# Wider search products, an earlier third key copy and loads asked for at written steps

## The chip, the cores and the metric

The kernel runs on one core of one Trainium2 chip. The metric is the device time of one execution in microseconds; several runs are shown by their median.

## The reference

Three stages follow one another. x goes through all of them, 3072 tokens (4 sequences of 768) by 384 numbers.

```python
# 1: linear attention with decay, 8 heads of 48, for each sequence
for t in range(768):
    state = alpha[:, :, t, :, None] * state + k[:, :, t] (outer) v[:, :, t]
    y[:, :, t] = q[:, :, t] @ state
# 2: dense layer, 384 -> 2048 -> 384
h = np.maximum(x @ w_in, 0.0);  x = h * h @ w_out
# 3: eight experts, 384 -> 1024 -> 384, each with room for cap = 3072 // 8 tokens
order = np.argsort(-(x @ w_gate).flatten())
for idx in order:
    tok, e = idx // 8, idx % 8
    if assigned[tok] >= 0 or counts[e] >= cap: continue
    assigned[tok] = e; counts[e] += 1
out[mask] = np.maximum(x[mask] @ w1[e], 0.0) @ w2[e]     # mask: tokens of e
```

## The kernel before, in words

**Attention** goes by 24 chunks of 128 tokens, six for each sequence. A chunk is the generator `attn`, which is called piece by piece. Its pieces: "p" and "a", two scans on VectorE (L233, L237); "q", the scaled keys and queries kt and qt; then sad, the decayed state (GpSimd, L253), and the scores psc (TensorE, L260); for chunks from the fourth on, `turn` (transposed keys pn, which ScalarE copies to kn, L299), `mask` (VectorE, L266), `update` (pu, TensorE, L307), `keep` (the new state, VectorE, L316 or L318) and `result` (TensorE: L278 with the state, L281 with the masked scores; ScalarE copies it out). The first chunk of a sequence has no L278, the last one no update. At its "q" piece a chunk asks for the load of the chunk after the next (L247 to L249), chunks 3 to 5 on the sync engine (SP), later ones on ScalarE.

**The dense layer** goes by eight units of three chunks (384 tokens), each in 16 steps of 128 hidden columns. A step has nine matmuls of ph (L415), ScalarE's and VectorE's work to make hl (the first unit's last part is VectorE's, L431), and, two steps later, nine matmuls of p (L443). Every factor is kept as a sum of two numbers, so each product has three parts. In the first 16 steps the weights are converted as well: a pair of slices comes as 64-bit integers, VectorE takes three operations for it (L382, L384, L386), ScalarE and GpSimd split it. The 17 pairs, the first and last in halves, are begun by `start_conv` and finished by a later call.

**The order** on TensorE, VectorE, ScalarE and GpSimd is written by hand in two regions, as the text runs. In the opening, `ORDER` lists it: "w" is a small matmul that only keeps TensorE busy, "0p" or "2n" the next piece of one of the first three chunks, "C" starts a conversion, "S" finishes it, "L" asks for the pairs that are due, "x" splits the first unit's x (L353, L354). Then `first_step(g)` runs for g from 0 to 17: ph, the conversion's end, hl, the next conversion's start, p of two steps ago, and a piece each of chunks 3 to 6, which begin in the steps that `BEGIN` names. SP is not among these engines. From step 18 on the order is the framework's own; `piece` calls the later chunks at a set rate, skipping two of their halts.

**The experts.** For each of seven experts a search finds the lowest logit that still gets a place: five iterations, each of which narrows the range 32-fold. An iteration compares all logits with 32 thresholds (cm, VectorE), counts by expert (pc, six matmuls, L892), takes the counts over as rc, adds the four groups of 32 rows (pb by `same`, four matmuls, L905), asks where an expert would be full (VectorE), and counts these thresholds (pb by `later`, L910):

```python
for g in range(G):
    pe.matmul(pb[0:T, 0:E], same[:, g * T:(g + 1) * T], rc[:, g * E:(g + 1) * E], ...)
full = sm.tile([T, E], BF, name="full", bufs=2)
dve.tensor_tensor(full, pb[0:T, 0:E], cap[0:T], op=OP.is_ge)
pe.matmul(pb[:, E:2 * E], later, full, start=True, stop=True)
```

Here T is 32, G 4 and E 8. At the end of a search pz (L931) gives what was taken. Then GpSimd gathers the expert's weights (`load_w`, w1s and w2s), ScalarE and VectorE or GpSimd split them (L974, L976), the tokens are gathered and turned (L984), and layer 1 (ph, L1011) and layer 2 (py, L1029) run, nine and three times three matmuls a step. The search for expert e+1, the gathers and splits stand between them where `PLAN` puts them, again in an order written by hand. The first search stands in `START` between the last unit's p matmuls (L694).

Of the kernel before, what the change touches and what calls it, by code (L numbers as in the profile page):

```python
# [7 lines left out]
F32 = mybir.dt.float32  # L8
# [24 lines left out]
T = 32  # L33
# [8 lines left out]
def table(entries):  # L42
    at = {}
    for r, p, what in entries:
# [19 lines left out]
         "1 A t 99 t 1 s 1 t x h0 B r d0 h1 r d1 r h2 p2 r open r h3 r h4 p3 h5 r r r x h6 r p4 p5 r r r p6").split()  # L64
LEAD = 4
RATE = 15 / 16
ORDER = ("w w w w w w w w w w 0p 0a 0q 1p 0s 0n w w 1a 0o w w 1q 2p 1s 1n 2a 2q 1o w 2s C S C L 2n w w 2o x w w w w "
         "w w w w w w w w S C L w").split()

PAIRS = [((0, 0), (0, 1)), ((0, 2), (1, 0))] + [((0, f + 2), (1, f)) for f in range(1, FT - 2)] + [((1, 14), (1, 15))]  # L70

BEGIN = 1, 5, 8, 12
SPLIT = (14, 14, 15)
SB = 2
WF = 3
# [11 lines left out]
def moe_kernel(ctx: ExitStack, tc: tile.TileContext, akq, v, w_in, w_out, w_gate, w1, w2, out,  # L87
# [105 lines left out]
    pool.iota(iopc[:, :, 1], pattern=[[1, NCH]], base=0, channel_multiplier=0, allow_small_or_imprecise_dtypes=True)  # L193
    onesb = consts.tile([128, 128], BF, name="onesb")
    trim = consts.tile([128, 128], BF, name="trim")
    later = consts.tile([T, 128], BF, name="later")
    same = consts.tile([128, 128], F16, name="same")
    iopw = iota([128, 1], [[0, 1]], base=-128 * ID0, cm=1, name="iopw")
    sel = consts.tile([16, E], F32, name="sel")

    def late_consts():
        pool.memset(onesb, 1.0)
        dve.tensor_scalar(trim, jp, 0.0, -1.0, op0=OP.is_gt, op1=OP.add)
        dve.tensor_scalar(later, ones[0:T], iop[0:T], 0.5, op0=OP.mult, op1=OP.is_gt)
        dve.tensor_copy(same, ident)
        dve.tensor_scalar(sel, jp[0:16, 0:E], -float(E), None, op0=OP.is_equal)
        dve.tensor_tensor(sel, sel, ident[0:16, 0:E], op=OP.add)

# [10 lines left out]
    def attn(ch, tags="aaaaa"):  # L219
# [24 lines left out]
            ae = ap_.tile([112, NP], F32, name="ae", bufs=2)  # L244
            pool.tensor_copy(ae, P[:, :, 0])
        yield "q"
        if CPU <= ch < NCH - 2:  # L247
            load(ch + 2, eng=sp if ch < 2 * CPU else act)
            load_v(ch + 2, sp if ch < 2 * CPU else act)  # L249
        if c:  # L250
# [69 lines left out]
        if ch >= CPU:  # L320
            kn2 = turn()
            yield "s"
            mask(0, NP)
            yield "m"
            pu = None if last else update()
            yield "u"
            if not last:
                keep(pu)
            result(0, NP)
            yield "o"  # L330
            return
        if late:
# [178 lines left out]
    def loads():  # L511
        while due:
            load_pair(due.pop(0))
# [74 lines left out]
        return n  # L588

    def piece():  # L590
        if next(att, None) in ("s", "u"):
            next(att)

    def first_step(g):


        u, f = steps[g]
        for i, at in enumerate(BEGIN):
            if g - at in (4, 5):
                go(early[i])  # L600
        ph = bank("h", "ph")
        gated, asked = tasks[:], tasks[:]
        del tasks[:]
        moe_a(u, f, ph)
        for t in asked:
            t.send(ph)

        old, hi = before[:], before_gate[:]
        del before[:], before_gate[:]
        for t in hi:  # L610
            next(t)
        for e in old:
            go(e, 2)
        while begun:
            go(begun.pop(0))
        for e in old:
            go(e)
        start_conv()
        if g >= 2:
            moe_b(0, g - 2)  # L620
        for t in tasks:
            next(t)
        for i, at in enumerate(BEGIN):
            if 0 <= g - at <= 4:
                go(early[i])
        for i, w in enumerate(SPLIT):
            if g == w:
                split_x(1, (i,))
        before.append(moe_ev(u, f, ph, mp_.tile([128, 2, UT], F32R, name="hl", bufs=3)))
        before_gate.extend(gated)  # L630
        loads()

    before, before_gate = [], []
    early = [attn(CPU + i) for i in range(len(BEGIN))]
# [95 lines left out]
    pool.iota(iot[:, 0], pattern=[[1, T]], base=0, channel_multiplier=0, allow_small_or_imprecise_dtypes=True)  # L730
    for i in range(1, ITERS):
        act.activation(iot[:, i], iot[:, i - 1], AF.Copy, scale=1.0 / T)
    iol = sm.tile([T, 1], F32, name="iol")
    act.activation(iol, iop[0:T], AF.Copy, scale=float(T) ** (1 - ITERS))
    ioslot = sm.tile([128, CAP], F32, name="ioslot")
    pool.iota(ioslot, pattern=[[1, CAP]], base=-int(OFF), channel_multiplier=0, allow_small_or_imprecise_dtypes=True)
    IDX, XG, RW = {}, {}, {}
# [116 lines left out]
    def search(k):  # L854
# [21 lines left out]
        for it in range(ITERS):  # L876

            pc = bank("a", "pc")
            thr = iot[:, 0]
            if it:  # L880
                thr = pc[:, G * E:G * E + T]
                dve.tensor_scalar(thr, iot[:, it], n, at, op0=OP.add, op1=OP.add)
            cm = sm.tile([128, NCH, T], BF, name="cm", bufs=2)
            dve.tensor_tensor(cm, m2[:, :, None].to_broadcast([128, NCH, T]),
                              thr[:, None, :].to_broadcast([128, NCH, T]), op=OP.is_ge)
            if it == 0:
                oh = sm.tile(eb, BF, name="oh", bufs=2)
                dve.tensor_tensor(oh, L, m[:, :, None].to_broadcast(eb), op=OP.is_equal)
            yield

            for c in range(0, NCH, G):
                pe.matmul(pc[:, 0:G * E], cm[:, c:c + G].rearrange("p c t -> p (c t)"),  # L892
                          oh[:, c:c + G].rearrange("p c e -> p (c e)"), start=c == 0, stop=c == NCH - G)
            rc = sm.tile([128, G * E], F16, name="rc", bufs=2)
            dve.tensor_copy(rc, pc[:, 0:G * E])
            if it == 1:
                ee = sm.tile(eb, F32, name="ee", bufs=1)
                dve.tensor_tensor(ee, oh, ioe[:, None, :].to_broadcast(eb), op=OP.mult)
            if it == 2:
                ei = sm.tile([128, NCH], F32, name="ei", bufs=2)  # L900
                dve.tensor_reduce(ei, ee, axis=AX.X, op=OP.add)
            yield
            pb = bank("a", "pb")
            for g in range(G):
                pe.matmul(pb[0:T, 0:E], same[:, g * T:(g + 1) * T], rc[:, g * E:(g + 1) * E], start=g == 0,  # L905
                          stop=g == G - 1)
            full = sm.tile([T, E], BF, name="full", bufs=2)
            dve.tensor_tensor(full, pb[0:T, 0:E], cap[0:T], op=OP.is_ge)
            yield
            pe.matmul(pb[:, E:2 * E], later, full, start=True, stop=True)  # L910
            if it == 1:
                at = n
            elif 1 < it < ITERS - 1:
                at2 = sm.tile([128, 1], F32, name="at", bufs=2)
                dve.tensor_scalar(at2, at, n, None, op0=OP.add)
                at = at2
            n0, n = n, sm.tile([128, 1], F32, name="n", bufs=4)
            steps = sm.tile([128, E], F32, name="steps", bufs=1)
            dve.tensor_scalar(steps, pb[:, E:2 * E], float(T) ** -it, None, op0=OP.mult, op1=OP.max, accum_out=n)
            yield  # L920

        hi = sm.tile([128, 1], F32, name="hi", bufs=2)
        dve.tensor_scalar(hi, n, n0, at, op0=OP.add, op1=OP.add)
        taken = sm.tile([T, E], F32, name="taken", bufs=2)
        dve.scalar_tensor_tensor(taken, n[0:T].to_broadcast([T, E]), iol, pb[0:T, 0:E], op0=OP.is_equal, op1=OP.mult)
        a = pb[:, 2 * E:2 * E + NCH]
        dve.tensor_scalar(a, m2, hi, None, op0=OP.is_ge)
        dve.copy_predicated(aid, a.bitcast(mybir.dt.uint32), ei)
        yield
        pz = bank("a", "pz")  # L930
        pe.matmul(pz[:, 0:E], ones[0:T], taken, start=True, stop=True)  # L931
        cl = sm.tile([128, E], F32, name="cl", bufs=2)
        dve.tensor_tensor(cl, cap, pz[:, 0:E], op=OP.subtract)
        cz = sm.tile([128, E], F32, name="cz", bufs=2)
# [379 lines left out]
```

## Time and profile before

| what | value |
|---|---|
| three runs | 862.66, 857.23, 861.27 us; median 861.27 |
| the profiled execution | 859.59 us, of which the profile's span is 857.3 us |
| mean granted clock of TensorE | 0.978 of full |
| TensorE busy | 812.6 us (95% of the span) |
| VectorE busy | 493.4 us (58%) |
| ScalarE busy | 338.0 us (39%) |
| GpSimd busy | 361.7 us (42%) |

The stages in the trace: the opening to 31 us, the 18 written steps to about 128 us, the free steps to about 530 us, the last unit with the first search to some 590 us, and the experts. Busy shares over the whole span mix these stages. In the rows below, PE is TensorE, PEld its weight loads, DVE VectorE, ACT ScalarE, POOL GpSimd and SP the sync engine. A row of a timeline names start and length in us, engine, line, operation, what it writes and reads with their shapes, and behind x how many instructions it joins; in brackets the engine's idle time ahead of it and what ended it.

### The profile page before, as it was taken

The numbers are of one execution on the slowest core, as the hardware profiler recorded it, in microseconds if no ns is written. First come the engines' busy times: TensorE is split into PE (matmuls) and PEld (weight loads), VectorE is DVE, ScalarE is ACT, GpSimd is POOL, SyncE is SP. The second block draws the span as 40 slices with busy tenths as digits, with TensorE's granted clock in tenths as the row PEclk, the third lists the DMA queues.
The fourth block names the chain that finished last, engine by engine and source line by source line (L and its number), as shares of the span: only waits on it lengthen the run. The fifth ranks groups of instructions, "written<-read, shape, count | busy, mean of one in ns | idle before, by whom it ended". The sixth has DMA issues, their size and how long they took to land.

```text
span 857.3 us, 14404 instructions
## 1 busy us (share of the span) xinstructions
PE 812.6 (95%) x5752; PEld 755.4 (88%) x5752; DVE 493.4 (58%) x1091; ACT 338.0 (39%) x616; POOL 361.7 (42%) x351
## 2 busy tenths in 40 slices
PE   7889989999999999999999999986999999999993
PEld 6889989999999999999999999866887888889993
DVE  8899993434435434435443123477877876877730
ACT  2455644333233233234233245123445435536620
POOL 2466633342243342243343245134557577572511
PEclk8899989999999999999999999998999999999997
DMA  8555421112112102112100000041441532523500
GB/s 240 169 180 191 160 75 39 54 37 71 54 38 95 51 24 92 45 41 80 51 8 29 7 29 1 15 157 38 175 164 41 203 124 80 203 81 123 203 28 30
DMA packets 21625, 75.53 MB, mean 88 GB/s; under 512 B 3137, under 2 KB 10178, under 8 KB 19634
## 3 DMA queue, kind: packets, MB, share of 16 engines
q0 software_dynamic: 5520, 34.61, 11.0%
q1 hardware_dynamic: 11682, 25.72, 9.5%
q10 hardware_dynamic: 4352, 14.24, 5.5%
q8 instruction: 46, 0.75, 0.4%
q14 instruction: 25, 0.20, 0.1%
HBM read 63.84 MB, written 9.54 MB: 86 GB/s over the span
## 4 chain that ended last, share of the span: by engine, by line
PE 72%; DVE 15%; ACT 5%; issue 4%; DMA 2%; POOL 0%; POOLq 0%; SPq 0%; DVEq 0%; ACTq 0%
PE ph L415 20%; PE p L443 19%; PE ph L1011 9%; PE py L1029 7%; ACT wbuf L974 3%; DVE wf L384 3%; DVE wbuf L976 3%; PE psc L260 3%; PE py L281 3%; PE p L694 2%; PE py L278 2%; DMA w1s<-in_moe_w_dram,wi 2%; DVE wf L382 1%; PE pu L307 1%; PE pn L296 1%
## 5 line engine op out<-in xcount | busy, mean ns | idle before, releaser
L415 PE MATMUL ph<-xT,wbuf 128*128 128x384 f32 x1152 | 226.3, 340 | 4.5 <-DVE hl L431 4.5
L415 PEld LDWEIGHTS ph<-xT,wbuf 128*128 128x128 f32 x1152 | 203.8, 188 | 7.5 <-DVE hl L431 5.4
L443 PE MATMUL p<-wbuf,hl 128*128 128x392 f32 (+1 forms) x1008 | 203.7, 346 | 0.0
L427 DVE SCALAR_TENSOR_TENSOR s<-ph,s 128x384 f32<-128x384 f32 x112 | 62.4, 557 | 229.6 <-ACT s L420 229.2
L443 PEld LDWEIGHTS p<-wbuf,hl 128*128 128x128 f32 x1008 | 177.8, 189 | 4.0 <-issue 3.0
L431 POOL TENSOR_TENSOR hl<-s,hl 128x384 fp32r<-128x384 f32 x96 | 97.4, 1014 | 187.8 <-ACT hl L428 177.8
L420 ACT ACTIVATE s<-ph 128x384 f32<-128x384 f32 x128 | 63.0, 492 | 176.4 <-PE ph L415 141.3
L1029 PE MATMUL py<-wbuf,hl 128*128 128x384 f32 x576 | 125.2, 347 | 0.0
L1011 PE MATMUL ph<-xt,wbuf 128*128 128x384 f32 x576 | 117.1, 346 | 1.4 <-DVE xt L986 0.9
L1011 PEld LDWEIGHTS ph<-xt,wbuf 128*128 128x128 f32 x576 | 98.9, 188 | 5.0 <-DVE xt L986 2.3
L1029 PEld LDWEIGHTS py<-wbuf,hl 128*128 128x128 f32 x576 | 99.0, 188 | 0.7
L428 ACT ACTIVATE hl<-s 128x384 fp32r<-128x384 f32 x96 | 50.4, 525 | 73.9 <-DVE s L427 73.9
L1019 ACT ACTIVATE hl<-ph 128x384 fp32r<-128x384 f32 x64 | 31.5, 493 | 113.1 <-PE ph L1011 105.6
L400 POOL TENSOR_TENSOR wbuf<-wf,wbuf 128x384 fp32r<-128x384 f32 x32 | 42.1, 1334 | 33.3 <-ACT wbuf L399 33.3
L1020 DVE SCALAR_TENSOR_TENSOR hl<-ph,hl 128x384 fp32r<-128x384 f32 x64 | 35.5, 556 | 35.2 <-ACT hl L1019 35.2
L974 ACT ACTIVATE wbuf<-w1s 128x1024 fp32r<-128x1024 f32 x24 | 52.1, 2215 | 2.6 <-DMA w1s<-in_moe_w_dram,wi 2.6
L1037 POOL DMA_INDIRECT out_dram<-o,idx x24 | 28.7, 1197 | 51.6 <-ACT o L1034 19.7
L976 POOL TENSOR_TENSOR wbuf<-w2s,wbuf 128x768 fp32r<-128x768 f32 x24 | 43.5, 1837 | 5.6 <-ACT wbuf L974 5.6
L253 POOL TENSOR_TENSOR sad<-state,ae 48x192 f32<-48x192 f32 x40 | 24.6, 614 | 41.7 <-DVE state L316 29.3
L782 POOL DMA_INDIRECT xg<-x2d,row x24 | 22.9, 954 | 38.8 <-DVE idx L838 14.9
L976 POOL TENSOR_TENSOR wbuf<-w1s,wbuf 128x1024 fp32r<-128x1024 f32 x11 | 32.9, 3020 | 2.9 <-ACT wbuf L974 2.8
L260 PE MATMUL psc<-qt,kt 48*128 48x128 f32 x384 | 28.8, 291 | 3.4 <-DVE qt L242 3.4
(211 smaller groups left out, 1058.7 us busy)
## 6 DMA issues: line engine op xcount, KB each, us to landing
akq<-in_akq_dram ACTq DMA_DIRECT2D x16, 677.2 KB, 4.6
raw<-in_moe_w_in_dram SPq DMA_DIRECT2D x16, 384.0 KB, 3.1
raw<-in_moe_w_out_dram SPq DMA_DIRECT2D x16, 384.0 KB, 3.8
x2d<-xo SPq DMA_DIRECT2D x24, 192.0 KB, 2.0
akq<-in_akq_dram SPq DMA_DIRECT2D x6, 677.2 KB, 8.1
v<-in_v_dram ACTq DMA_DIRECT2D x16, 192.0 KB, 2.4
v<-in_v_dram SPq DMA_DIRECT2D x8, 192.0 KB, 4.9
xf<-xf SPq DMA_DIRECT2D x16, 72.0 KB, 2.6
```

Source lines behind the costliest of these rows:

```text
L260: pe.matmul(psc[j][:, p * 128:(p + 1) * 128], kt[o:o + D, p], qt[o:o + D, p], start=True, stop=True)
L400: pool.tensor_tensor(to[1], x, to[0].bitcast(F32), op=OP.subtract)
L415: pe.matmul(ph[:, :UT], win[:, wi, kt, fs], XT[u][:, xi, kt, :], start=n == 0, stop=n == 3 * KT - 1)
L420: act.activation(s, ph[:, :UT], AF.Relu)
L427: dve.scalar_tensor_tensor(s, ph[:, :UT], 0.0, s, op0=OP.max, op1=OP.mult)
L428: act.activation(hl[:, 0], s, AF.Copy)
L431: (dve if u == 0 or (u, f) == (NU - 1, FT - 1) else pool).tensor_tensor(hl[:, 1], s, hl[:, 0].bitcast(F32), op=OP.subtract)
L443: pe.matmul(PY[u][t][:, :w], hl[:, si, t * C:(t + 1) * C], wout[:, wi, f, :w], start=f == 0 and n == 0, stop=f == FT - 1 and n == 2)
L974: act.activation(dst[:, 0], src, AF.Copy)
L976: (dve if "d" in e else pool).tensor_tensor(dst[:, 1], src, dst[:, 0].bitcast(F32), op=OP.subtract)
L1011: pe.matmul(ph[:, :CAP], wa[:, wi, kt, j, :], xt[:, xi, kt, :], start=n == 0, stop=n == 3 * KT - 1)
L1029: pe.matmul(PX[k, i][:, :DM], hl[:, hi_, i * 128:(i + 1) * 128], wb[:, wi, j, :], start=j == 0 and n == 0, stop=j == FT2 - 1 and n == 2)
```

## The change

`ORDER` takes "2n" (the third chunk's transposed keys and their copy) ahead of the first two conversions, starts a third conversion behind "L" instead of far later, and has one "w" fewer there. The loads of chunks 7 and 8 leave the "q" pieces of chunks 5 and 6 and are asked for on SP at the end of steps 15 and 17. For chunks from the fourth on `result` goes ahead of `update`, and the halt between them is gone, so chunks 3 to 6 take six pieces where they took seven. In the search `same` and `later` have 128 columns and 128 rows: the sum over groups and all that follows stands in 128 rows, of which `later` uses the first 32; pz has 128 rows too. `same` becomes four matrices of 128 by 128, made by GpSimd ahead of the search.

```diff
@@ -64,12 +64,14 @@
          "1 A t 99 t 1 s 1 t x h0 B r d0 h1 r d1 r h2 p2 r open r h3 r h4 p3 h5 r r r x h6 r p4 p5 r r r p6").split()
 LEAD = 4
 RATE = 15 / 16
-ORDER = ("w w w w w w w w w w 0p 0a 0q 1p 0s 0n w w 1a 0o w w 1q 2p 1s 1n 2a 2q 1o w 2s C S C L 2n w w 2o x w w w w "
-         "w w w w w w w w S C L w").split()
+ORDER = ("w w w w w w w w w w 0p 0a 0q 1p 0s 0n w w 1a 0o w w 1q 2p 1s 1n 2a 2q 1o w 2s 2n C S C L C w 2o x w w w w "
+         "w w w w w w w w S L w").split()
 
 PAIRS = [((0, 0), (0, 1)), ((0, 2), (1, 0))] + [((0, f + 2), (1, f)) for f in range(1, FT - 2)] + [((1, 14), (1, 15))]
 
 BEGIN = 1, 5, 8, 12
+
+LATER = {7: 15, 8: 17}
 SPLIT = (14, 14, 15)
 SB = 2
 WF = 3
@@ -193,16 +195,17 @@
     pool.iota(iopc[:, :, 1], pattern=[[1, NCH]], base=0, channel_multiplier=0, allow_small_or_imprecise_dtypes=True)
     onesb = consts.tile([128, 128], BF, name="onesb")
     trim = consts.tile([128, 128], BF, name="trim")
-    later = consts.tile([T, 128], BF, name="later")
-    same = consts.tile([128, 128], F16, name="same")
+    later = consts.tile([128, 128], BF, name="later")
     iopw = iota([128, 1], [[0, 1]], base=-128 * ID0, cm=1, name="iopw")
     sel = consts.tile([16, E], F32, name="sel")
 
     def late_consts():
         pool.memset(onesb, 1.0)
         dve.tensor_scalar(trim, jp, 0.0, -1.0, op0=OP.is_gt, op1=OP.add)
-        dve.tensor_scalar(later, ones[0:T], iop[0:T], 0.5, op0=OP.mult, op1=OP.is_gt)
-        dve.tensor_copy(same, ident)
+
+        dve.tensor_scalar(scratch, iop, 0.5, None, op0=OP.is_gt)
+        dve.scalar_tensor_tensor(scratch, iop, T - 0.5, scratch, op0=OP.is_lt, op1=OP.mult)
+        dve.tensor_scalar(later, ones, scratch, None, op0=OP.mult)
         dve.tensor_scalar(sel, jp[0:16, 0:E], -float(E), None, op0=OP.is_equal)
         dve.tensor_tensor(sel, sel, ident[0:16, 0:E], op=OP.add)
 
@@ -244,7 +247,7 @@
             ae = ap_.tile([112, NP], F32, name="ae", bufs=2)
             pool.tensor_copy(ae, P[:, :, 0])
         yield "q"
-        if CPU <= ch < NCH - 2:
+        if CPU <= ch < NCH - 2 and ch + 2 not in LATER:
             load(ch + 2, eng=sp if ch < 2 * CPU else act)
             load_v(ch + 2, sp if ch < 2 * CPU else act)
         if c:
@@ -322,11 +325,10 @@
             yield "s"
             mask(0, NP)
             yield "m"
-            pu = None if last else update()
-            yield "u"
+
+            result(0, NP)
             if not last:
-                keep(pu)
-            result(0, NP)
+                keep(update())
             yield "o"
             return
         if late:
@@ -588,7 +590,7 @@
         return n
 
     def piece():
-        if next(att, None) in ("s", "u"):
+        if next(att, None) == "s":
             next(att)
 
     def first_step(g):
@@ -621,7 +623,7 @@
         for t in tasks:
             next(t)
         for i, at in enumerate(BEGIN):
-            if 0 <= g - at <= 4:
+            if 0 <= g - at <= 3:
                 go(early[i])
         for i, w in enumerate(SPLIT):
             if g == w:
@@ -629,6 +631,10 @@
         before.append(moe_ev(u, f, ph, mp_.tile([128, 2, UT], F32R, name="hl", bufs=3)))
         before_gate.extend(gated)
         loads()
+        for ch, at in LATER.items():
+            if g == at:
+                load(ch)
+                load_v(ch)
 
     before, before_gate = [], []
     early = [attn(CPU + i) for i in range(len(BEGIN))]
@@ -730,8 +736,12 @@
     pool.iota(iot[:, 0], pattern=[[1, T]], base=0, channel_multiplier=0, allow_small_or_imprecise_dtypes=True)
     for i in range(1, ITERS):
         act.activation(iot[:, i], iot[:, i - 1], AF.Copy, scale=1.0 / T)
-    iol = sm.tile([T, 1], F32, name="iol")
-    act.activation(iol, iop[0:T], AF.Copy, scale=float(T) ** (1 - ITERS))
+    iol = sm.tile([128, 1], F32, name="iol")
+
+    same = sm.tile([128, G, 128], F16, name="same")
+    pool.tensor_copy(same.rearrange("p g (r t) -> p g r t", t=T),
+                     ident.rearrange("p (g t) -> p g t", g=G)[:, :, None, :].to_broadcast([128, G, 128 // T, T]))
+    act.activation(iol, iop, AF.Copy, scale=float(T) ** (1 - ITERS))
     ioslot = sm.tile([128, CAP], F32, name="ioslot")
     pool.iota(ioslot, pattern=[[1, CAP]], base=-int(OFF), channel_multiplier=0, allow_small_or_imprecise_dtypes=True)
     IDX, XG, RW = {}, {}, {}
@@ -902,10 +912,10 @@
             yield
             pb = bank("a", "pb")
             for g in range(G):
-                pe.matmul(pb[0:T, 0:E], same[:, g * T:(g + 1) * T], rc[:, g * E:(g + 1) * E], start=g == 0,
+                pe.matmul(pb[:, 0:E], same[:, g], rc[:, g * E:(g + 1) * E], start=g == 0,
                           stop=g == G - 1)
-            full = sm.tile([T, E], BF, name="full", bufs=2)
-            dve.tensor_tensor(full, pb[0:T, 0:E], cap[0:T], op=OP.is_ge)
+            full = sm.tile([128, E], BF, name="full", bufs=2)
+            dve.tensor_tensor(full, pb[:, 0:E], cap, op=OP.is_ge)
             yield
             pe.matmul(pb[:, E:2 * E], later, full, start=True, stop=True)
             if it == 1:
@@ -921,14 +931,14 @@
 
         hi = sm.tile([128, 1], F32, name="hi", bufs=2)
         dve.tensor_scalar(hi, n, n0, at, op0=OP.add, op1=OP.add)
-        taken = sm.tile([T, E], F32, name="taken", bufs=2)
-        dve.scalar_tensor_tensor(taken, n[0:T].to_broadcast([T, E]), iol, pb[0:T, 0:E], op0=OP.is_equal, op1=OP.mult)
+        taken = sm.tile([128, E], F32, name="taken", bufs=2)
+        dve.scalar_tensor_tensor(taken, n.to_broadcast([128, E]), iol, pb[:, 0:E], op0=OP.is_equal, op1=OP.mult)
         a = pb[:, 2 * E:2 * E + NCH]
         dve.tensor_scalar(a, m2, hi, None, op0=OP.is_ge)
         dve.copy_predicated(aid, a.bitcast(mybir.dt.uint32), ei)
         yield
         pz = bank("a", "pz")
-        pe.matmul(pz[:, 0:E], ones[0:T], taken, start=True, stop=True)
+        pe.matmul(pz[:, 0:E], ones, taken, start=True, stop=True)
         cl = sm.tile([128, E], F32, name="cl", bufs=2)
         dve.tensor_tensor(cl, cap, pz[:, 0:E], op=OP.subtract)
         cz = sm.tile([128, E], F32, name="cz", bufs=2)
```

## Rows read from the trace of the kernel before

**Rows 1.** Stretches: window us; busy us (instructions) PE, PEld, DVE, ACT, POOL; PEclk; DMA; GB/s.

```profile
60.00:113.00 53.00, 51.85 (x406) 49.75 (x406) 52.08 (x65) 31.52 (x73) 31.54 (x26) 1.00 0.49 159
113.00:128.00 15.00, 12.81 (x93) 11.72 (x93) 13.71 (x21) 4.59 (x11) 6.02 (x9) 0.77 0.36 107
150.00:300.00 150.00, 150.00 (x1102) 142.74 (x1100) 67.41 (x111) 49.43 (x101) 51.52 (x64) 1.00 0.19 57
651.20:684.60 33.40, 32.49 (x238) 28.20 (x237) 25.45 (x86) 16.05 (x21) 20.22 (x15) 1.00 0.35 129
```

**Rows 2.** Timeline of the opening, TensorE and then VectorE.

```profile
25.23 1.65 PE L278 MATMUL py<-qt,sad 112*128 112x128 f32 x6 [1.90 <-ACT kn L299]
...
29.09 0.74 DVE L316 TENSOR_TENSOR state<-pu,sad 48x192 f32<-48x192 f32 x2 [2.71 <-PE pu L307]
...
31.74 1.35 DVE L382 TENSOR_SCALAR wf<-raw 128x768 int32<-128x768 int32 x1
...
34.12 0.96 DVE L386 SCALAR_TENSOR_TENSOR wf<-raw,wf 128x768 int32<-128x768 int32 x1
```

**Rows 3.** SP's sixth v load; steps 15 and 16 on VectorE and TensorE.

```profile
29.01 0.33 SPq L134 DMA_DIRECT2D v<-in_v_dram  x1
...
114.01 2.04 DVE L233 TENSOR_TENSOR_SCAN suf<-akq,fresh 112x516 f32<-112x516 f32 x1
...
118.39 0.53 DVE L431 TENSOR_TENSOR hl<-ph,hl 128x384 fp32r<-128x384 f32 x1
...
118.97 2.19 PE L415 MATMUL ph<-xT,wbuf 128*128 128x384 f32 x9 [2.19 <-DVE hl L431]
...
122.09 3.23 PE L443 MATMUL p<-wbuf,hl 128*128 128x384 f32 x9
```

**Rows 4.** TensorE's timeline, a chunk with update and then one without.

```profile
320.98 0.56 PE L307 MATMUL pu<-v,kn 128*48 128x48 f32 x16
321.47 1.16 PE L278 MATMUL py<-qt,sad 112*128 112x128 f32 x8
322.56 1.08 PE L281 MATMUL py<-Pt,v 128*48 128x128 f32 x16
...
233.09 1.75 PE L415 MATMUL ph<-xT,wbuf 128*128 128x384 f32 x9
234.67 1.05 PE L278 MATMUL py<-qt,sad 112*128 112x128 f32 x8
235.66 1.08 PE L281 MATMUL py<-Pt,v 128*48 128x128 f32 x16
```

**Rows 5.** TensorE's timeline, a search's iteration in an expert period, and a wait in the same.

```profile
658.00 0.32 PE L892 MATMUL pc<-oh,cm 128*128 128x32 bf16 x6
658.16 0.78 PE L1029 MATMUL py<-wbuf,hl 128*128 128x384 f32 x3
658.90 0.24 PE L905 MATMUL pb<-rc,same 128*32 128x8 f16 x4
659.07 0.80 PE L1029 MATMUL py<-wbuf,hl 128*128 128x384 f32 x3
659.80 0.17 PE L910 MATMUL pb<-full,later 32*128 32x8 bf16 x1
659.90 1.84 PE L1011 MATMUL ph<-xt,wbuf 128*128 128x384 f32 x9
661.58 0.69 PE L1029 MATMUL py<-wbuf,hl 128*128 128x384 f32 x3
...
682.36 0.32 PE L892 MATMUL pc<-oh,cm 128*128 128x32 bf16 x6 [0.63 <-DVE cm L884]
```

**Rows 6.** Weight loads by line (ns min/median/max), and GpSimd's first gather.

```profile
L905 PEld LDWEIGHTS <-same x140: 92/93/107, 547.2 to 759.3; 128*32 128x32 f16 x140
L892 PEld LDWEIGHTS <-cm x210: 95/96/151, 546.9 to 758.4; 128*128 128x128 bf16 x105
...
566.62 1.16 POOL L760 DMA_INDIRECT w1s<-in_moe_w_dram,wi  x1 [26.71 <-DVE b L796]
```

## The prediction

> **What bounds the kernel now.** I read the table of stretches first, by stage. Each stage has another limit. From 60 to 113 us, while the conversions and the first seven chunks run, VectorE is busy 52.08 of 53 us: it sets the pace, and TensorE waits for it now and then. From 150 to 300 us TensorE is busy all 150 us, with no gap. In one whole expert period, 651.2 to 684.6 us, TensorE is busy 32.49 of 33.4 us, so it is the bound by the busy time, yet VectorE, ScalarE and the gathers hand it work at a few fixed points. And from 113 to 128 us the granted clock was 0.77 of full on average, so part of that stretch ran at 1.2 GHz [rows 1]. So each edit is priced in its own stage. After the stretches I read the timeline of each engine at the places the diff names, for the idle time in brackets and what ended it.
>
> **Third chunk and third conversion.** In the opening order TensorE waits 1.90 us (to 25.23) for ScalarE's copy kn of the third chunk. That copy stands behind ScalarE's first conversion, which waits for VectorE. VectorE itself then has nothing from 26.38 to 29.09 (2.71 us idle, ended by pu), and converts pair 1 only at 31.74, taking until 35.08 [rows 2]. The edit puts "2n" ahead of the conversions and the third "C" right behind the second. So kn no longer waits, pu ends some 1.8 us earlier, and the 3.3 us of pair 1's conversion goes into the hole. On VectorE, the bound of this stage, nothing is added or removed; the hole of 2.71 us is filled. Pair 1's data must be there at 26.38: its buffer is free once the third chunk's products are made, well before. One warm matmul fewer goes, in a place where TensorE waits anyway: nothing. What is late next is state and the split of x, now behind the conversion, but pair 1's 3.3 us come off their successor. The gain is passed on as long as VectorE is without a gap, which it is to 113 us [rows 1], and TensorE behind it loses nothing later. Bounds: 0 (loads of the next pairs come late instead) to 3.3; I take 2.7, the measured hole.
>
> **The two loads.** Chunk 7's load was SP's already; it is now written down at step 15, not 11. Chunk 8's moves from ScalarE (step 15) to SP (step 17). SP is not among the engines whose order is written by hand, and the trace shows that it does not follow the text: the sixth v load, written in the fourth step, was issued at 29.01, before the first step, as soon as its buffer was free [rows 3, 2]. So I expect both loads about where they were, and nothing queued behind a wait on SP: by then all weight pairs have been asked for. ScalarE is rid of two issues of about 0.3 us (the length of one on SP [rows 3]) while it waits for TensorE. What this edit might touch is the stumble behind it: VectorE takes chunk 7's scan at 114.01 ahead of the step's hl, which comes only at 118.39; TensorE waits 2.19 us for it and runs the next nine p matmuls in 3.23 us, about twice their usual time [rows 3, 1]. Unless the scan goes elsewhere this stays. I take 0, between -2 and +4.
>
> **Update behind result.** For chunks from the fourth on, result's matmuls now come ahead of update's, and the halt between mask and update is gone (the pieces per chunk stay five). TensorE's work is the same, but the shapes are joined otherwise. Before: full array (ph), 48 columns (pu), full (L278), 48 columns (L281), full. After: full, full (L278), 48 columns for both L281 and pu, full. A change of shape costs time: L278 behind pu takes 1.09 us (321.47 to 322.56), behind ph 0.99 (234.67 to 235.66) [rows 4]. The second switch saved, ph to pu, I price the same: 0.2 us a chunk. In the gapless stage there are fourteen updates (chunks 7 to 22 without 11 and 17, which end a sequence and have none); chunks 12 and 18 begin a sequence and have no L278, so twelve gain: 2.4 us, carried whole, because TensorE is without a gap there [rows 1]. The state's update comes later by result's two microseconds; its reader, the next chunk's product on GpSimd, comes several steps later. Bounds 0 to 2.9 (twice that switch in all fourteen, rounded); I take 2.4. Chunks 3 and 4 lie under VectorE: nothing.
>
> **Search on the full array.** The diff keeps the count of matmuls: in each of 35 iterations four by same and one by later, in 7 searches a pz. It changes 32 columns or 32 rows into 128, so they no longer switch the array's shape. Price of one iteration now: three py matmuls ahead of same take 0.74 us (658.16 to 658.90), four by same 0.17, three py 0.73, one by later 0.10, nine ph 1.68 (to 661.58). Undisturbed, nine take 1.58 (233.09 to 234.67), three 0.53. The excess is 0.21 + 0.17 + 0.20 + 0.10 + 0.10 = 0.78 us. Five matmuls in the full shape would take 0.13, as pc's six take 0.16 (658.00 to 658.16), and pc's own switch of number format, and that of the new ones, leave a quarter of a microsecond: I count 0.4 saved [rows 4, 5]. With 35 iterations and an estimate of 0.2 for each pz (two switches at the 0.1 of later's) this is about 15 us of TensorE time.
>
> Most of it comes back as waits. In one period two iterations stand ahead of the pc at 682.36, for which TensorE already waits 0.63 us because VectorE is behind with conversions and cm [rows 5]. What TensorE saves ahead of it adds to that wait: 0.8 lost of 2.0. Of the three iterations behind it, 1.2 us, each answer of VectorE (rc, full, cm) has to come sooner too; between none and all, I take half, 0.6. Five whole periods give 3.0; the first search, with the last unit's matmuls as filling, and the second, ahead of its gather, 0.5 each. Sum 4.0; bounds 1 (the first searches alone) and 9 (all but what the 682.36 wait takes).
>
> The loads of the weights get 128 columns for 32. The trace has both: 93 ns for same's 32 columns, 96 for the 128 of cm [rows 6]. That is 3 ns in 140 loads, 0.4 us at most. The Trainium skill ("TensorE: Matmul & The Clock Gate", section on LDWEIGHTS) says otherwise: load time grows with the columns, P / 1.2 ns, so by an estimate from that page 80 ns more for each of the 140, 11 us, and little would be left of the search's gain. The rows speak against it here.
>
> Constants: later takes three small VectorE instructions for one, same's cast leaves VectorE; together below 0.3 us, under TensorE's slow stretch. The new same, 512 numbers a row, is made by GpSimd, which is idle 26.71 us before the first gather at 566.62 [rows 6]: nothing; with that cover gone, about 1 us.
>
> **Sum.** 2.7 + 0 + 2.4 + 4.0 = 9.1 us off the profiled execution's 859.59: 850.5. The three runs have a mean 0.8 above that execution (median 861.27), so 851.3.
>
> **Rivals.** (a) The stumble at 114 to 128 goes, because chunk 7's scan no longer stands ahead of hl: 2.19 of waiting and 1.5 of slow p, near 4 us [rows 3]; 847. For it: the loads are written later, and the order of free instructions is made anew. Against it: SP's habit above. (b) The search keeps nearly all but the 682.36 loss: 9 for 4; 846. For it: TensorE is busy 97% of a period. Against: VectorE's share is 76% and its answers are in line with TensorE's own work. (c) The change does not do what it is said to do: switches shrink, waits grow by as much, and the head's hole opens again behind TensorE: search 1, head 1, update 2.4; 856. The wait at 682.36 speaks for it. (d) Loads as long as their columns: 11 of 15 us are taken back, search 1; 854. This is what the Trainium skill's rule on LDWEIGHTS, weighed above, would make of the change; [rows 6] speak against it. (e) Slower: chunk 7's or 8's scan stands in VectorE's queue ahead of an hl while its load, now really asked for at step 15 or 17, is still on the way. The engine can't pass it; each such halt costs TensorE what the stumble costs, 4 to 6 us with its slow clock, and two or three of them, 12 in all, outweigh the gains: 863. It decides when SP obeys the step and the scan is still placed early. The sixth v load speaks against it.
>
> **How the numbers follow.** Forecast 45%, (a) 18%, (b) 12%, (c) 15%, (d) 3%, (e) 7%. A measurement of this kernel tells about 1% from no change: below 852.7 is faster, above 869.9 slower. The forecast, with its own bounds of 3 us, lies below 852.7 in about 6 of 10 (27%); with (a) and (b) this makes 57%. Over 869.9 only a bad (e): 3%. Range: 844 takes in (a), (b) and a little below; 859 takes in (c), (d) and an update or head worth nothing; out are (e) and the far ends.
>
> **What would show it.** After: no wait of TensorE for kn near 25, no hole of VectorE behind 26, ph of step 0 about 2 us earlier; L278 right behind ph at 0.99; same's and later's matmuls with 128 by 128 and the py behind them at undisturbed length; the wait for cm in each period longer by nearly a microsecond; the stumble near 112 to 125 as before. The prediction is wrong if the scans of chunks 7 and 8 change place, if the expert period falls by over 1 us, or if the opening's gain is gone by 113 us.

## Result and profile after

The change takes 847.69 us (median of 846.45, 846.51, 848.87 and 848.94) for 861.87 before: 0.9846 of it, with an interval of 0.9806 to 0.9887. A second comparison gave 846.96 for 860.03, 0.9842 (0.9825 to 0.9858). So 13 to 14 us are gained. The forecast was 851.3, about 10 us below the median it started from; the time lies in the range, but one term of the sum, the update's, was clearly too small.

The profiled execution took 846.45 us, with a span of 844.7. Its stretches, as in [rows 1]:

```profile
60.00:113.00 53.00, 52.19 (x416) 50.57 (x412) 52.05 (x64) 32.35 (x74) 30.79 (x27) 1.00 0.49 160
113.00:128.00 15.00, 11.56 (x94) 10.78 (x93) 11.52 (x21) 7.09 (x18) 6.13 (x10) 1.00 0.28 81
150.00:300.00 150.00, 150.00 (x1088) 145.89 (x1087) 65.05 (x106) 52.96 (x107) 53.14 (x64) 1.00 0.18 54
...
567.50:581.30 13.80, 8.38 (x53) 7.61 (x49) 9.00 (x24) 5.91 (x8) 10.53 (x6) 0.51 0.19 58
...
640.55:673.86 33.31, 31.10 (x237) 27.66 (x237) 25.98 (x87) 16.09 (x21) 23.33 (x15) 1.00 0.36 132
```

The limits are the same as before, but in the expert period TensorE now stands idle for 2.2 us where it stood for 0.9, and the period takes 33.31 us for 33.4: this one alone keeps next to nothing of what TensorE saves (others keep more, see the part on why). The stretch from 113 to 128 us has the full clock; e5, the same program again, shows that this does not come with the change.

The opening, TensorE and then VectorE; beside [rows 2]:

```profile
23.72 0.94 PE L281 MATMUL py<-qt,sad 112*128 112x128 f32 x6 [0.40 <-ACT kn L302]
...
31.05 2.42 PE L417 MATMUL ph<-xT,wbuf 128*128 128x384 f32 x8 [1.98 <-DVE xT L356]
...
26.51 0.55 DVE L384 TENSOR_SCALAR wf<-raw 128x768 int32<-128x768 int32 x1
...
28.09 1.64 DVE L388 SCALAR_TENSOR_TENSOR wf<-raw,wf 128x768 int32<-128x768 int32 x1
```

The wait for kn is 0.40 us for 1.90, and pair 1's conversion (26.51 to 29.73) fills VectorE's hole. TensorE waits 1.98 us for the split of x instead, which stands behind it, as forecast. Steps 15 and 16, beside [rows 3]: SP asks for chunk 8's load at 110.58; the scan still stands ahead of hl, and TensorE waits as long as before, yet runs the next p matmuls at their usual pace.

```profile
110.58 0.34 SPq L133 DMA_DIRECT2D akq<-in_akq_dram  x1
...
110.48 2.04 DVE L236 TENSOR_TENSOR_SCAN suf<-akq,fresh 112x516 f32<-112x516 f32 x1
...
115.42 1.85 PE L417 MATMUL ph<-xT,wbuf 128*128 128x384 f32 x9 [2.17 <-DVE hl L433]
...
117.69 1.83 PE L445 MATMUL p<-wbuf,hl 128*128 128x384 f32 x9
```

A chunk with update on TensorE, beside [rows 4]. L278, L281 and L307 of before are L281, L284 and L310 here. From the first of them to the end of pu it is 2.35 us (312.80 to 315.15); the same matmuls took 2.59 (320.98 to 323.57), and the ph ahead of them lost 0.1 more:

```profile
311.21 1.75 PE L417 MATMUL ph<-xT,wbuf 128*128 128x384 f32 x9
312.80 1.05 PE L281 MATMUL py<-qt,sad 112*128 112x128 f32 x8
313.79 1.08 PE L284 MATMUL py<-Pt,v 128*48 128x128 f32 x16
314.70 0.53 PE L310 MATMUL pu<-v,kn 128*48 128x48 f32 x16
315.15 1.15 PE L445 MATMUL p<-wbuf,hl 128*128 128x392 f32 x5
```

An iteration of a search, and the two longer waits of that period, beside [rows 5]:

```profile
647.30 0.77 PE L1039 MATMUL py<-wbuf,hl 128*128 128x384 f32 x3
647.92 0.24 PE L915 MATMUL pb<-rc,same 128*128 128x8 f16 x4
648.03 0.78 PE L1039 MATMUL py<-wbuf,hl 128*128 128x384 f32 x3
648.64 0.18 PE L920 MATMUL pb<-full,later 128*128 128x8 bf16 x1
648.68 1.81 PE L1021 MATMUL ph<-xt,wbuf 128*128 128x384 f32 x9
650.33 0.69 PE L1039 MATMUL py<-wbuf,hl 128*128 128x384 f32 x3
...
653.28 0.17 PE L799 MATMUL pp<-mi,onesb 128*128 128x24 bf16 x1 [0.98 <-DVE wi L768]
...
671.90 0.31 PE L902 MATMUL pc<-oh,cm 128*128 128x32 bf16 x6 [1.16 <-DVE cm L894]
```

From the py ahead of same to the py behind ph it is 3.03 us (647.30 to 650.33) for 3.42: 0.39 saved, the 0.4 of the forecast. The wait for cm went from 0.63 to 1.16 us.

**Stages.** One trace against one trace misleads here, so the stages are compared over all traces. Their marks are these starts (of the change; the same instructions in the others): first conversion, steps 3, 15 and 19, last unit, second expert, seventh expert.

```profile
22.91 0.35 DVE L384 TENSOR_SCALAR wf<-raw 128x384 int32<-128x384 int32 x1
...
42.43 0.44 PE L417 MATMUL ph<-xT,wbuf 128*128 128x384 f32 x1 [0.99 <-DVE hl L433]
...
107.22 0.42 PE L417 MATMUL ph<-xT,wbuf 128*128 128x384 f32 x1
...
129.69 0.34 PE L417 MATMUL ph<-xT,wbuf 128*128 128x384 f32 x1
...
528.09 0.33 PE L700 MATMUL p<-wbuf,deferred 128*128 128x384 f32 x1
...
612.21 0.42 PE L1021 MATMUL ph<-xt,wbuf 128*128 128x384 f32 x1
...
772.65 0.34 PE L1021 MATMUL ph<-xt,wbuf 128*128 128x384 f32 x1
```

| us between marks | before | e1 search | e2 order | e3 update | e4 loads | change | e5 again | e6 |
|---|---|---|---|---|---|---|---|---|
| conversion to step 3 | 22.33 | 21.32 | 18.93 | 21.25 | 21.25 | 19.52 | 19.73 | 19.11 |
| step 3 to 15 | 65.72 | 65.67 | 65.69 | 64.54 | 65.20 | 64.79 | 64.77 | 65.71 |
| step 15 to 19 | 24.72 | 24.56 | 24.66 | 22.66 | 25.90 | 22.47 | 24.26 | 22.89 |
| step 19 to last unit | 402.99 | 402.94 | 402.97 | 398.40 | 402.97 | 398.40 | 398.40 | 402.99 |
| last unit to 2nd expert | 84.03 | 83.02 | 87.48 | 85.90 | 84.62 | 84.12 | 85.03 | 83.08 |
| 2nd to 7th expert | 162.75 | 161.74 | 165.31 | 165.03 | 165.95 | 160.43 | 161.08 | 160.05 |

The third, fifth and sixth rows differ by 1.7 to 3.5 us between executions with the same code in them; the fourth agrees within 0.05. Between the two first traces alone the search would seem to be worth 2.2 us, since the trace of before had the shortest expert periods of all with the old search.

### The profile page after: what moved, and what is told of

Its sections match the earlier page's. It is cut to its first block, busy times and chain, and to the rows that moved or that the text cites. A ratio compares the mean times of both kernels' runs of the same rounds, so it can differ in the third digit from the quotient of the medians.

```text
span 844.7 us, 14407 instructions
## 1 busy us (share of the span) xinstructions
PE 794.6 (94%) x5750; PEld 750.0 (89%) x5750; DVE 492.6 (58%) x1092; ACT 340.6 (40%) x616; POOL 362.5 (43%) x352
## 4 chain that ended last, share of the span: by engine, by line
PE 72%; DVE 8%; ACT 2%; DMA 2%; issue 1%; POOL 0%; POOLq 0%; ACTq 0%
PE ph L417 21%; PE p L445 19%; PE ph L1021 9%; PE py L1039 8%; DVE wbuf L986 3%; PE p L700 2%; PE psc L263 2%; PE py L284 2%; DMA w1s<-in_moe_w_dram,wi 2%; PE py L281 2%; ACT wbuf L984 2%; DVE cm L894 1%; PE pc L902 1%; DVE hl L1030 1%; PE pn L299 1%
```

## Experiments

Ratios are to the kernel before, on the same chip.

**e1 to e4: one part of the change each.** The diffs are the hunks of the change.

```diff
e1: -    pe.matmul(pb[0:T, 0:E], same[:, g * T:(g + 1) * T], ...   +    pe.matmul(pb[:, 0:E], same[:, g], ...
    (and later, full, iol, taken, pz)
e2: -  2s C S C L 2n w w 2o x w w w w ... S C L w                  +  2s 2n C S C L C w 2o x w w w w ... S L w
e3: -  update, halt, keep, result                                  +  result, keep(update())
e4: +LATER = {7: 15, 8: 17}
```

> Only the search's part of the change is made (128 columns and rows for same, later, pz). Theory A, switches saved and mostly turned into waits: up to the last unit's first matmul nothing moves (within 0.3 us); from there to the end 3.5 us are saved, or about 2.3 if TensorE's clock again stays low for longer around the second search; TensorE's waits for VectorE in the search (cm, mk, rc, full) together grow by 4 to 6 us. Rival B, the search is the larger part of the measured gain: 7 us or more from there to the end. Rival C, swallowed whole: under 1 us. As nothing ahead of the search is changed, the granted clock from 113 to 128 us should again be near 0.77, if what happens there belongs to the program.

Measured: 855.8 us, 0.9937 (0.9904 to 0.9971), so 5.4 us. By the table, five periods take 160.8 us on average with the new search (e1, change, e5, e6) and 164.8 with the old (before, e2 to e4), and last unit to second expert 83.8 for 85.5: 5.6 us. This is between theories A and B: more than the trace of before let expect. By its interval, e1's time alone leaves room for 2.5 to 8 us, and last unit to second expert overlaps (83.0 to 85.0 new, 84.0 to 87.5 old), so these 1.7 us are not shown to be the search's. The clock from 113 to 128 us fell again, as in before.

> Only the opening's written order is changed. Theory A, the hole of VectorE is filled and VectorE carries the gain: the first matmul of step 3 comes 2.6 us earlier than before, that of step 15 by 2.6 to 3.0. Rival B, the opening's part is the whole 3.5 us that the full change has at step 15: 3.5. Rival C, the gain is lost again under the conversions: below 1 us at step 15. What follows step 16 depends on whether the clock falls there: 2.5 to 5 us at step 19.

Measured: 860.16, 0.998 (0.9951 to 1.0009). Conversion to step 3 takes 18.9 us, on average 19.3 in the four traces with the new order and 21.5 in the four with the old: 2.2 us, good to some tenths, as stretches of half clock lie in this stage too (0.50 of full from 25 to 31 us in before). From there to step 15 the order changes nothing (65.69). Theory A, a little small; the time alone does not tell it from nothing.

> Only result is put ahead of update, with the halt taken out. Theory A, each shape switch costs both the matmul ahead of it and the one behind it, and two are saved for each chunk: 0.33 us a chunk in twelve chunks and 0.2 in the two that begin a sequence, 4.4 us from step 19 to the last unit, and some 0.3 us for each of the chunks 3 and 4 before that, so 0.6 at step 15. Rival B, the forecast's price: 2.4 us in the free steps and nothing ahead of them. Opening and search as before.

Measured: 854.59, 0.9924 (0.9892 to 0.9956), some 6.5 us. Step 19 to last unit loses 4.57 us, steps 3 to 15 some 0.9 (64.77 in e5 for 65.71 in e6, which differ in this order alone; 1.2 in this trace). Theory A; the forecast's 2.4 falls.

> Only the loads of chunks 7 and 8 are moved to the sync engine. Theory A, they change nothing that TensorE waits for: TensorE still waits about 2.2 us for the step's hl behind the scan of chunk 7, the clock falls behind it as before, and all milestones stand within 0.5 us of before. Rival B, the loads are why the stretch from 113 to 128 us lost 2.2 us less in the full change: about 2 us are gained between steps 15 and 19, and the clock stays at 1.00. Rival C: a scan waits for a late load, 2 us or more are lost there.

Measured: 861.27, 0.999 (0.9966 to 1.0014). The wait at step 16 is there, and behind it a longer stretch of half clock than before had: TensorE's row in the timeline, and the stretch in the table of stretches (columns as in [rows 1]); 0.50 of full is 1.2 GHz:

```profile
116.13 3.25 PE L417 MATMUL ph<-xT,wbuf 128*128 128x384 f32 x9 [2.17 <-DVE hl L433]
```

```profile
115.37:125.61 10.24, 9.48 (x54) 9.02 (x56) 8.65 (x18) 0.98 (x2) 2.02 (x5) 0.50 0.24 69
```

So the loads gain nothing that the time shows, and the full clock of the change's first trace is not theirs. Steps 3 to 15 are 0.5 us shorter here (65.20), but not in e6 with the same loads (65.71).

**e5: the whole change again.**

> The whole change once more, for a second trace and more times. Theory A, the parts add and the differences between single traces are stretches of half clock and answers of VectorE that come late in some executions: 13 to 15 us below the median of before; the stages without such stretches (first conversion to step 3, 19.5; step 3 to step 15, 64.8; step 19 to the last unit, 398.4 us) come out the same within 0.5 us, those with them (step 15 to 19; last unit to the eighth layer-1 group) differ by 1 us or more. Rival B, what the first trace showed belongs to the program: all stages the same within 0.5 us, and no half clock behind the wait at step 16.

Measured: 846.96, 0.9842. Theory A: the same 2.17 us of wait at step 16, but here p's nine matmuls behind it take 3.23 us, and steps 15 to 19 are 24.26 us for 22.47.

```profile
115.40 2.29 PE L417 MATMUL ph<-xT,wbuf 128*128 128x384 f32 x9 [2.17 <-DVE hl L433]
...
118.62 3.23 PE L445 MATMUL p<-wbuf,hl 128*128 128x384 f32 x9
```

**e6: update ahead of result, without the halt.**

```diff
-            result(0, NP)
             if not last:
                 keep(update())
+            result(0, NP)
```

> The whole change, but with update's matmuls ahead of result's again, in the same piece (the halt stays out). Theory A, the gain of this part is shape switches and nothing else: 4.6 us come back between step 19 and the last unit (403.0 for 398.4) and 0.9 between steps 3 and 15; the time is 4 to 6 us above that of the change. Rival B, the gain is the missing halt, that is the place of update and of the state's sum among the steps: nothing comes back. Rival C, the forecast's price of one sided switches: 2.4 us come back.

Measured: 853.91, 0.9935, for 846.96 of e5 beside it. Step 19 to last unit is 402.99 again, steps 3 to 15 65.71. The whole gain of this part is the order of the two groups of matmuls; the halt is worth nothing. TensorE's rows have the old steps again, 1.08 us from L281 to L284 for 0.99:

```profile
314.05 1.75 PE L417 MATMUL ph<-xT,wbuf 128*128 128x384 f32 x9
315.73 0.56 PE L310 MATMUL pu<-v,kn 128*48 128x48 f32 x16
316.23 1.16 PE L281 MATMUL py<-qt,sad 112*128 112x128 f32 x8
317.31 1.08 PE L284 MATMUL py<-Pt,v 128*48 128x128 f32 x16
```

**e7 and e11: chunk 7's scans written into the steps**, behind hl (e7 from step 16, e11 from step 15), and chunk 9's load on SP.

```diff
+    seventh = attn(CPU + len(BEGIN))
+        if g >= FT:          # e11: FT - 1
+            go(seventh)
```

> The whole change, and chunk 7's two scans are written into the last two ordered steps, behind hl of steps 15 and 16, with chunk 9's load on the sync engine. Theory A, TensorE's wait of 2.2 us at step 16, and the half clock that follows it in most traces, come from these scans standing ahead of hl: the wait is gone, the clock stays at 1.00 to step 19, and steps 15 to 19 take 19 to 21 us for 22.5 (24.7 before); the time is 2 to 5 us below the change. Rival B, the scans are only late then: chunk 7's scores come late in the free steps and TensorE waits there for as long: no gain. Rival C, another engine is as late as VectorE there (ScalarE's hl): the wait shrinks by under 1 us.

> As the kernel with chunk 7's scans written into the steps, but one step earlier: the first scan at the end of step 15 (in a hole of VectorE of 1.7 us behind hl), the second at the end of step 16, the scaled keys at the end of step 17. Theory A, both the wait of TensorE at step 16 and the lateness that took its gain away in the free steps go: steps 15 to 19 take 18 to 19 us (22.5 and 24.3 in the change), steps 19 to the last unit 398.4 to 400, the time is 3 to 6 us below the change. Rival B, the free steps are late again, because VectorE has the scans of two chunks ahead of their s there: 402 us or more for steps 19 to the last unit, no gain.

Measured: e7 849.99, 0.9887 (e5 beside it 846.96); e11 848.25, 0.9874. In both the wait at step 16 is gone and the clock stays full there; step 18 comes 2.7 us earlier after step 15 than in the change's first trace (15.5 for 18.2). By step 22 both are 1.9 and 2.2 us behind that trace, level with e5 within 0.5. Rival B: the wait only moves. In e7 TensorE waits 0.97 us for VectorE, 0.69 for ScalarE and 0.45 for GpSimd between 123 and 127.1 us, and the granted clock is 0.53 from 134.4 to 138.0; why its times lie 3 us above e5's is not shown. In e11 the later wait is for GpSimd: its sad, 0.6 us apiece in the mean, runs beside VectorE's scans of 122.86 to 125.64 and takes 3.03 us for two, the splits behind it are late, and TensorE waits 2.85 us for them. The eight p matmuls behind it then run at half clock (0.50 from 128.0 to 131.3 us).

```profile
122.91 3.03 POOL L256 TENSOR_TENSOR sad<-state,ae 48x192 f32<-48x192 f32 x2
...
122.86 1.23 DVE L236 TENSOR_TENSOR_SCAN suf<-akq,fresh 112x516 f32<-112x516 f32 x1 [0.58 <-POOL ae L248]
...
124.35 1.29 DVE L240 TENSOR_TENSOR_SCAN A<-akq,whole 112x515 f32<-112x515 f32 x1
...
127.81 2.83 PE L445 MATMUL p<-wbuf,hl 128*128 128x392 f32 x8 [2.85 <-POOL wbuf L651]
```

**e8: the first slice of w1s split by GpSimd.**

```diff
-EXTRA = ((4, 2, "h0"), (4, 4, "h1"), (5, 3, "d0 h2"), ...
+EXTRA = ((4, 2, "h0"), (4, 4, "h1"), (5, 3, "p0 h2"), ...
```

> The whole change, and the first slice of w1s is split by GpSimd and not by VectorE in the periods that have the common plan (four or five of them). Theory A, the wait for cm of the third iteration (1.2 us a period in the change) stands behind that split of 2.2 us on VectorE and eats what the wider products save: it falls below 0.3 us, and the time is 3 to 5 us below the change. Rival B, VectorE waits for GpSimd while GpSimd's three us of subtracting run, or GpSimd's later splits come late for layer 1: the wait only moves, and the time is within 1 us of the change, or above it.

Measured: 863.0, 1.0041 (1.0027 to 1.0055), 16 us above e5. The wait for cm is gone, but the next expert's first matmuls wait up to 3.89 us for GpSimd, which needs 8.75 us for three slices and then 7.17 for the rest:

```profile
650.70 2.29 PE L1021 MATMUL ph<-xt,wbuf 128*128 128x384 f32 x6 [3.89 <-POOL wbuf L986]
...
641.89 8.75 POOL L986 TENSOR_TENSOR wbuf<-w1s,wbuf 128x1024 fp32r<-128x1024 f32 x3
650.61 7.17 POOL L986 TENSOR_TENSOR wbuf<-w2s,wbuf 128x768 fp32r<-128x768 f32 x4
```

So the 2.2 us on VectorE are the reason of the wait for cm, as theory A has it, and GpSimd has no room to take them: rival B, and worse. The first period, in which nothing waits for GpSimd, shows what the split costs: 31.3 us for 32.6 in the change.

**e10: the third conversion alone moved.**

```diff
-... 1o w 2s 2n C S C L C w 2o x ...
+... 1o w 2s C S C L C 2n w 2o x ...
```

> The whole change, but the third chunk's key copy stands behind the conversions again; the third conversion keeps its new place. Theory A, the opening's gain is that VectorE's hole is filled by the third conversion, wherever the key copy stands: first conversion to step 3 takes 19 to 20 us, as in the change (18.9 to 19.7), and the time is that of the change. Rival B, the earlier key copy is the gain: 21.3 us, as with the order of before. Rival C, both: 20.3.

Measured: 847.41, 0.9857; conversion to step 3 19.3 us. Theory A. TensorE waits 2.13 us for kn again and nothing is lost: the early "2n" is worth nothing.

```profile
24.90 0.94 PE L281 MATMUL py<-qt,sad 112*128 112x128 f32 x6 [2.13 <-ACT kn L302]
```

**e9 and e12: small matmuls into the waits of the second search.** Their results are not used. The half clock there lasts: from 567.50 to 581.30 us in the change's trace the granted clock is 0.51, near 1.2 GHz (the stretches above).

```diff
-... "1 A t 99 t 1 s 1 t x h0 B r d0 h1 r d1 r h2 p2 r open r h3 r h4 ...
+... d1 " + "w " * 18 + "r h2 p2 " + "w " * 11 + "r open r h3 " + "w " * 10 + "r h4 ...    (e12: 10, 7, 6)
```

> The whole change, and 39 small matmuls (128 columns of ones, results unused) are put where TensorE waits for the splits of the first expert's weights in the second search: 18 ahead of the first iteration's same, 11 ahead of later, 10 ahead of the second iteration's counts. Theory A, TensorE's clock falls there because it stands idle for 2.7, 1.8 and 1.6 us in a row, and the half clock (6.8 to 13.7 us long in the traces so far) then meets the turning of the tokens and the first layer-1 matmuls: no half clock between the last unit and the fifth layer-1 group, that stretch (79.8 and 80.8 us in the two traces of the change, last unit to eighth group) takes 76 to 78 us, and the time is 1.5 to 4 us below the change. Rival B, the clock falls all the same: no gain. Rival C, the small matmuls make the search's own matmuls late: 1 to 3 us slower.

> The whole change with 10, 7 and 6 small matmuls for 18, 11 and 10, since each took 0.23 us in the run before and they overran the waits by 1.4, 0.8 and 0.7 us. Theory A, they fit into the waits now (2.3 of 2.7 us, 1.6 of 1.8, 1.4 of 1.6) and still keep the clock at 1.00: last unit to eighth layer-1 group takes 77 to 78 us for 79.8 to 80.8, the time is 2 to 3 us below the change. Rival B, the idle time that is left is enough for the clock to fall: 80 us, no gain.

Measured: e9 847.51, 0.9872; e12 847.73, 0.9829 (0.9797 to 0.986). In both the clock is 1.00 all through (e9: 566 to 577 us), and the first layer-1 matmuls take 1.81 us for the 3.11 of the change:

```profile
566.00:577.00 11.00, 9.92 (x100) 9.60 (x99) 6.87 (x10) 7.29 (x6) 9.19 (x6) 1.00 0.44 135
```

```profile
582.34 1.81 PE L1022 MATMUL ph<-xt,wbuf 128*128 128x384 f32 x9
```

```profile
578.39 3.11 PE L1021 MATMUL ph<-xt,wbuf 128*128 128x384 f32 x9
```

(First e9's stretch, then e9's timeline, last the change's timeline.) Yet neither is faster than the change. In e9 the small matmuls overran the waits (4.26 us ahead of same, where the change's trace has a wait of 2.72). In e12, whose trace is of its slowest execution (851.35), they fit. There the fifth layer-1 group comes 61.9 us after the last unit's mark for 64.6 in the change, but the ninth 83.7 for 84.1, since TensorE waits 2.28 us for cm in the first period; in the third it waits 1.76 us for GpSimd's split. No version beat the change by more than the measurement can tell.

## Why the prediction was right or wrong

**Third chunk and third conversion**: 2.7 forecast, 2.2 measured. Right in mechanism: the hole is filled and VectorE carries the gain to step 15. e10 shows that the conversion alone does it; the earlier key copy, which the prediction counted in, has no part in it.

**Loads**: 0 forecast, 0 measured (e4). SP asked for chunk 8's load at 110.58, ahead of step 16, so it does not keep to the written step 17. The stumble stayed, as said, and rival (a) fell: only the clock behind it differs, and no run links that to the change.

**Update behind result**: 2.4 forecast with bounds of 0 to 2.9, 5.5 measured (4.57 + 0.9). The step that failed is "a change of shape costs time: ... 1.09, behind ph 0.99", taken for all of a switch. That is only what the matmuls behind the switch lose; those ahead of it lose as much. The rows of before had it: ph ahead of pu takes 1.69 us (319.29 to 320.98), ahead of L278 1.58 (233.09 to 234.67) [rows 4]. Two switches a chunk, both sides, are 0.33 us in the chunks shown; twelve chunks make 4.0.

The two chunks that begin a sequence (12 and 18) are a control. They have no L278, so both orders have two switches, and from ph through the p behind pu and L281 both take 4.75 us (255.97 to 260.72 before, 248.79 to 253.54 in the change). They still gain 0.17 us each, but behind that: in before and in e6 the load of p's weights waits 0.22 us there for VectorE's copy of the logits (at 262.37 and 388.97 in before), in the change it does not. The prediction was right to leave them out of the switches. So 4.57 us are twelve chunks of 0.33 to 0.36 and two such waits. The Trainium skill ("TensorEngine Tiling (Array Packing)", section Key Properties) says that a change of tiling mode drains TensorE; the rows agree in that both neighbours lose time, and put about 0.17 us on one change here. That it is a drain they do not show.

"Chunks 3 and 4 lie under VectorE: nothing" failed too: 0.9 us. VectorE is busy 52.08 and 52.05 of 53 us there in the two traces, but TensorE is busy too, 51.85 and 52.19; a full VectorE alone was no proof that TensorE has room.

**Search**: 4.0 forecast, 5.4 measured by e1's times, within the bounds of 1 and 9. The main point was right, that most of TensorE's saving comes back as waits. The iteration shown saves the 0.39 us of the price. A whole period of five iterations saves 1.6 us of TensorE's busy time and keeps 0.7. These are two periods without late answers (columns as in [rows 1]; before, then after):

```profile
651.16:684.51 33.35, 32.44 (x238) 28.15 (x237) 25.45 (x86) 16.05 (x21) 20.17 (x15) 1.00 0.35 128
612.21:644.83 32.62, 30.84 (x239) 27.61 (x238) 25.49 (x86) 15.96 (x22) 19.69 (x13) 1.00 0.37 134
```

In such periods the wait for cm grows by 0.5 to 0.6 us, where 0.8 was forecast, and that for pp from 0.28 to 0.56, which the forecast did not have; e8 shows what cm stands behind. Four periods of 0.7 and the fifth, 28.9 us for 29.1, make 3.1 us: the 3.0 of the forecast. The 3.9 of the table is more because in three of the four traces with the old search, and in one of the four with the new, the sums by `same` or `later` wait 0.5 to 1.6 us in two or three of the periods, mostly for a late rc of VectorE, as here in e2:

```profile
680.01 0.24 PE L905 MATMUL pb<-rc,same 128*32 128x8 f16 x4 [1.43 <-DVE rc L895]
```

VectorE itself stands idle for 2.18 us ahead of that rc, and the profile names no engine as the cause. Neither what makes these answers late nor whether the wider products make them rarer is shown. So the term was sized about right for the periods, and what it is worth ahead of them stays open. The 15 us of TensorE time were too many: TensorE is busy 800.7 us in e1 for 812.6. The quarter of a us that the price left to changes of number format is there (the excess in the iteration of the change is 0.39 us, of which 0.13 are the five matmuls), but that the format is its cause no run shows. A weight load of same takes 96 ns with 128 columns for 93 with 32, as forecast:

```profile
L915 PEld LDWEIGHTS <-same x140: 95/96/107, 536.7 to 746.9; 128*128 128x128 f16 x140
```

Rival (d) falls with it.

**The sum** is 2.2 + 0 + 5.5 + 5.4 = 13.1 for 9.1, and 13 to 14 were measured. That the time came out below the forecast is owed to the update, 3.1 us more than forecast, and not to luck with (a) or (b); for the search's 1.4 more the noise of its time leaves it open.

## What to carry to other kernels

A switch of the array's shape costs both neighbours: read the matmuls ahead of it and behind it against the same ones undisturbed, and join equal shapes where TensorE has no gap; here all of it was kept there. Where TensorE waits for answers, less than half of such savings remained (0.7 of 1.6 us a period), and moving work to another helper only moved the wait (e8, e11). When executions differ by stretches of half clock and by late answers, compare stages over several traces, and periods without them, before believing a stage's difference.

## What had not been expected of the hardware

The same wait of 2.17 to 2.19 us at step 16 was followed by no half clock in two traces (change, e8), and by 10.2 us of it in e4, where the clock fell while the wait still lasted; p's nine matmuls took 1.83 or 3.23 us for it in two executions of one program (change, e5). Why the clock falls in one and not in another stays open.

GpSimd and VectorE seem to hold each other up. In the change's trace a sum of 8 numbers a row takes 0.59 us in one period, for 0.17 in its other periods, and ends as GpSimd's subtraction does (652.49); this lengthens the wait for pp to 0.98 us:

```profile
645.25 7.24 POOL L986 TENSOR_TENSOR wbuf<-w2s,wbuf 128x768 fp32r<-128x768 f32 x4
...
651.92 0.59 DVE L947 SCALAR_TENSOR_TENSOR ez<-cz,ioe 128x8 f32<-128x8 f32 x1
```

The Trainium skill ("SBUF — State Buffer", section Who interferes with whom) tells of a pair of ports that the two share under an exclusive lock. These rows agree with it, and so do e11's, where GpSimd's two sad take 3.03 us beside VectorE's scans and 1.08 in the change without them; but the DMA engines were busy too in e11 (0.99 from 124 to 126 us), and no run separates the two.
